# One product for two heads' tails, the reciprocal's argument on ScalarE, and another set of priorities

## The chip, the cores and the metric

The kernel runs on one core of a Trainium2 chip. Its engines work side by side, each through its own queue in order: TensorE (PE in the profile, its weight loads PEld), VectorE (DVE), ScalarE (ACT), GpSimd (POOL), and SyncE (SP), which here only issues DMAs. The metric is the device time of one execution in microseconds, as the median of the timed runs.

## The reference

Three stages follow one another. Attention with 4 batches, 8 heads, 576 positions and head dimension 64: of each row of scores only the 32 largest are kept.

```python
scores = scale * np.matmul(q, k.transpose(0, 1, 3, 2))
kth = np.partition(scores, -top_k, axis=-1)[..., -top_k:-top_k + 1]
scores = np.where(scores >= kth, scores, -1e9)
attn = np.exp(scores - np.max(scores, axis=-1, keepdims=True))
attn = attn / (np.sum(attn, axis=-1, keepdims=True) + 1e-09)
x = np.matmul(attn, v)                       # then heads side by side: 2304 rows of 512
x = np.maximum(np.maximum(x @ w1, x @ w2), x @ w3) @ w_out   # first MoE, 512 -> 768 -> 512
# second MoE: softmax over 8 experts' logits, each row to its best expert:
out[row] = gate[row] * (np.maximum(x[row] @ w1[e], 0) @ w2[e])
```

## The kernel before, in words

Attention works in 72 units. A "full" unit is 128 queries (a block j of 0 to 3) of one pair of heads p; there are 64 of them. A "comb" unit holds the last 64 queries of two pairs; there are 8. The 576 keys fall into four chunks of 128 (KC = 4) and a tail of 64 (TL = 64).

Per unit the steps are: load and split the queries (`q_load`, `q_split`, `q_prep`), TensorE makes scores (`scores`, L751), ScalarE copies them (`s_copy`, L762), VectorE folds the two halves of a row (L820) and finds the 32nd largest by rounds of MAX8 and MATCH_REPLACE8 (L828, L832, L835, L854). `mask` (L874 on ScalarE, L876 on GpSimd) and `expo` (L882 on ScalarE) give weights and, through the accumulator, their sums; `recip` prepares the sum on GpSimd (L937: plus 1e-9, times a scale) and takes its reciprocal on VectorE (L936); from unit 14 on (`early_scale`) GpSimd scales the rows by it (`scale_rows`, L946). `pt` transposes the weights on TensorE (L899, and L913 for both heads' tails at once), ScalarE copies them out (L903, L921).

`av` is the product with v. In a full unit it writes both heads into one PSUM tile, head 0 in partitions 0 to 63 and head 1 in 64 to 127. First come the tails, one product for each head in a quarter of the array (L963, 64 rows by 64 columns), then four chunks by two heads (L967, 128 rows by 64 columns). An f32 product is two records in the trace. `norm` copies the result to the tile xf (L1001), and `x_split` makes two f16 parts of it (L1028, L1033), the input of the first MoE.

v lies in a tile of five slots by two heads (`v_load`, five DMAs for each pair of heads, tile bufs = 5): four chunks, and a slot for the tail, where head 1's tail is loaded twice, once in the lower and once in the upper partitions.

The first MoE (`moe1_steps`) runs on groups of 128 to 320 queries, two a batch and three for the last one; its products (`mm`, L1079, L1119) and evictions (`ev`, L1085, L1088, L1094, L1099) are mixed in with later attention units, and the last groups run alone at the end. Its weights are loaded, decoded and split in the first 150 us (`weight_steps`, steps f, with a check g, L477 and L479). `route_early` computes routing tables for the first three batches (L1383 to L1473) while the last units run. After that come the experts of the second MoE (L1646, L1667).

Up to there the order of work on each engine is made by a planner (`Plan`). Each `add(engine, length, f, reads, writes)` is a step with an assumed length in ns; the planner goes through time and gives each free engine, of the steps that are ready, the one with the smallest key. The key is the step's number in the list less the value of `SOON` under the name of the function that added it; a larger value means sooner. The order is written out; on the chip each engine keeps it and waits where its inputs are late. `at(name, tenant, part, bufs)` names a buffer that a step uses; a new tenant waits until an old one has left.

Of the kernel before, what the change touches and what calls it, by code (L numbers as in the profile page):

```python
# [10 lines left out]
F32 = mybir.dt.float32  # L11
# [5 lines left out]
AF = mybir.ActivationFunctionType  # L17
# [134 lines left out]
def moe_chain_kernel(  # L152
# [112 lines left out]

    xscale = const.tile([128, B + 1, 4], F32, name="xscale")
    REDO = B
# [44 lines left out]
    def whole(redo):  # L312
# [308 lines left out]
        def v_load(b, p):  # L621
            for i, hd in ((0, 0), (0, 1), (1, 0), (1, 1), (2, 1)):
                def f(i=i, hd=hd):
                    if (b, p) not in VT:
                        VT[b, p] = ap_.tile([128, NTT, 2, D], F32, name="v", bufs=5)
                    vt, src = VT[b, p], of_batch(v, b)[2 * p + hd]
                    if i == 0:
                        nc.sync.dma_start(vt[:, 0:KC, hd, :], src[0:KC * 128].rearrange("(c p) d -> p c d", p=128))
                    elif i == 1:
                        nc.sync.dma_start(vt[:TL, KC, hd, :], src[KC * 128:S])  # L630
                    else:
                        nc.sync.dma_start(vt[TL:128, KC, hd, :], src[KC * 128:S])
                add("SP", ISSUE, f, (), [at("v", (b, p), (i, hd), 5)], size=(131072, 16384, 16384)[i])

        def v_max(b):
# [5 lines left out]
            for i in range(4):  # L641
# [11 lines left out]
            add("DVE", 60, lambda: V.tensor_scalar(xscale[:, b, 2:3], xscale[:, b, 1:2], float(2.0 ** -13), None, op0=OP.mult),  # L653
                [at("xs", 0, (b, 0))], [at("xs", 0, (b, 2))])

        def x_descale(b):
# [75 lines left out]
        def bat(u):  # L732
            return u[1]
# [197 lines left out]
        def recip(u):  # L931
            sm, r = at("sm", u, None, 3), at("r", u, None, 2)

            def f():
                RR[u] = ap_.tile([128, 2], F32, name="r", bufs=2)
                V.reciprocal(RR[u], SUM[u])  # L936
            add("POOL", 348, lambda: G.tensor_scalar(SUM[u], SUM[u], 1e-9, xscale[:, bat(u), 2:3], op0=OP.add, op1=OP.mult),  # L937
                [at("xs", 0, (bat(u), 2))], [sm])
            add("DVE", 71, f, [sm], [r])
# [9 lines left out]
        def av(u):  # L949
# [4 lines left out]
            def f():  # L954
                r = RR.pop(u)
                pst = psM.tile([128, 512], F32, name="m")
                ps = pst[:, 0:256].rearrange("p (a b) -> p a b", a=2)
                if full:
                    p = u[3]
                    vt = VT[b, p]  # L960
                    for hd in range(2):
                        rows = slice(hd * TL, (hd + 1) * TL)
                        PE.matmul(ps[rows, 0, :], vt[rows, KC, hd, :], PT[u, 2][rows, 0, :], start=True, stop=False,  # L963
                                  skip_group_check=True)
                    for c in range(KC):
                        for hd in range(2):
                            PE.matmul(ps[hd * 64:(hd + 1) * 64, 0, :], vt[:, c, hd, :], PT[u, hd][:, c, :],  # L967
                                      start=False, stop=(c == KC - 1), skip_group_check=True)
# [3 lines left out]
                else:  # L972
                    for g in range(2):
                        vt = VT[b, u[2] + g]
                        for hd in range(2):
                            o = ps[hd * 64:(hd + 1) * 64, 0, g * TL:(g + 1) * TL]
                            for c in range(KC):
                                PE.matmul(o, vt[:, c, hd, :], PT[u, g][:, c, hd * TL:(hd + 1) * TL],
                                          start=(c == 0), stop=False, skip_group_check=True)
                            PE.matmul(o, vt[:TL, KC, hd, :], PT[u, 2][:TL, g, hd * TL:(hd + 1) * TL],  # L980
                                      start=False, stop=True, skip_group_check=True)
# [5 lines left out]
            vs = [at("v", (b, p), None, 5) for p in ((u[3],) if full else (u[2], u[2] + 1))]  # L987
            add("PE", (1400 if full else 2700) + (0 if early_scale(u) else 230), f,
                vs + [pt_at(u, i) for i in range(3)] + ([] if early_scale(u) else [at("r", u, None, 2)]), [T])

# [4 lines left out]
        def norm(u):  # L995
# [3 lines left out]
            def f():  # L999
                XF[u] = ap_.tile([128, 128], F32, name="xf", bufs=2)  # L1000
                A.activation(XF[u], AV.pop(u)[:, 0, :], AF.Copy)  # L1001
# [5 lines left out]
            def h():  # L1007
                XF[u] = ap_.tile([128, 128], F32, name="xf", bufs=2)
                G.tensor_tensor(XF[u], box["rb"][:, 0, :], box["rb"][:, 1, :], op=OP.mult)
# [46 lines left out]
        def moe1_steps(g):  # L1056
# [72 lines left out]
            for j, off, m in g["tiles"]:  # L1129
# [44 lines left out]
        EARLY = 67  # L1174
        SOON = {"prefetch_first": 215, "q_prep": 190, "k_prep": 130, "scores": 120, "setup_routing": 120, "k_split":
                95, "first_expert": 95, "q_split": 90, "s_copy": 80, "x_split": 70, "g": 60, "pt": 45, "f": 25, "ev": 20,
                "av": 20, "fin": 5, "mask": -5, "expo": -15, "norm": -25, "v_max": -25, "weight_scales": -35, "setup_bias":
                -35, "scale_rows": -45, "q_load": -60, "route_early": -65, "k_load": -70, "mm": -75, "v_load": -105}
        LAG, LAST, STOP = 3, 1, 0
# [615 lines left out]
```

## Time and profile before

| | |
|---|---|
| median of 3 runs | 1018.72 us (1018.18 to 1021.07) |
| the profiled execution | 1023.0 us |
| its span, first to last instruction | 1021.1 us |
| TensorE busy | 924.2 us (91%) |
| VectorE busy | 752.5 us (74%) |
| ScalarE busy | 699.3 us (68%) |
| GpSimd busy | 548.6 us (54%) |
| mean granted TensorE clock | 0.939 |

Busy time is a union: overlapping records of an engine count once. A mean over the span hides the stages, and so the rows below are cut by stage. "Idle before" is the time in which an engine had nothing running ahead of an instruction, and "<-" names what ended it.

### The profile page before, as it was taken

To read this page: it belongs to the slowest core of one execution; us is meant where nothing else is said; L and a number is where in the kernel's file an instruction comes from. 1 tells how busy PE (TensorE), PEld (TensorE's weight loads), DVE (VectorE), ACT (ScalarE), POOL (GpSimd) and SP (SyncE) were. 2 spreads that over 40 slices of the span, in tenths; PEclk is the share of its full clock that TensorE was granted. 3 is DMA by queue.
4 is the path that set the end of the run, shared out by engine and by line. 5 is a ranking of instruction groups with operands and counts; after the bars stand their busy time and mean duration, and the time that the engine had idled before them with its cause. 6 is when DMAs were issued, how large, how long until landed. Compare 5 with 4: busy or idle time off the path is not lost. (4 is left out here: it accounts for less than half of the span.)

```text
span 1021.1 us, 21954 instructions
## 1 busy us (share of the span) xinstructions
PE 924.2 (91%) x7518; PEld 769.0 (75%) x7518; DVE 752.5 (74%) x2510; ACT 699.3 (68%) x1624; POOL 548.6 (54%) x831
## 2 busy tenths in 40 slices
PE   5357599999999999999999999998899899989995
PEld 4245478887778888778888887875797678768883
DVE  7999989999999999999989999996327111331110
ACT  7889889899888999888989888765432222432221
POOL 4678568787767786776876776654210211221000
PEclk8568689999999999999999999998899899989998
DMA  7743230132201123000001000000301521241000
GB/s 188 209 133 108 66 95 16 32 92 66 77 14 33 41 46 100 7 17 30 17 20 40 29 10 2 27 1 9 122 13 53 197 63 42 73 157 50 25 22 27
DMA packets 83795, 60.48 MB, mean 59 GB/s; under 512 B 67009, under 2 KB 67009, under 8 KB 83650
## 3 DMA queue, kind: packets, MB, share of 16 engines
q1 hardware_dynamic: 80770, 49.32, 17.0%
q0 software_dynamic: 2880, 9.44, 2.7%
q8 instruction: 65, 1.06, 0.4%
q14 instruction: 80, 0.66, 0.2%
HBM read 49.30 MB, written 9.44 MB: 58 GB/s over the span
## 5 line engine op out<-in xcount | busy, mean ns | idle before, releaser
L828 DVE MAX8 tk<-wk 128x8 f32<-128x288 f32 x576 | 237.2, 446 | 0.0
L876 POOL TENSOR_TENSOR ss<-mk,ss 128x576 f32<-128x576 bf16 x144 | 185.7, 1297 | 45.5 <-ACT mk L874 44.8
L835 DVE MATCH_REPLACE8 wk<-tk,wk 128x288 f32<-128x288 f32 x432 | 188.2, 441 | 0.0
L874 ACT ACTIVATE mk<-ss,kb 128x576 bf16<-128x576 f32 x144 | 110.6, 780 | 19.2 <-POOL kb L777 19.0
L1647 ACT ACTIVATE hid<-ph 128x512 f32<-128x512 f32 x36 | 21.5, 598 | 140.5 <-PE ph L1646 140.5
L882 ACT ACTIVATE ss<-ss,kb 128x576 f32<-128x576 f32 x144 | 112.0, 779 | 2.8 <-POOL ss L876 2.6
L751 PE MATMUL s<-ks,qt 128*128 128x288 f32 x512 | 95.1, 330 | 19.6 <-ACT ss L762 19.6
L762 ACT ACTIVATE ss<-s 128x576 f32<-128x576 f32 x144 | 93.8, 651 | 21.5 <-PE s L751 20.5
L820 DVE TENSOR_TENSOR wk<-s,ss 128x576 f32<-128x576 f32 x144 | 102.7, 744 | 5.6 <-ACT ss L762 5.6
L946 POOL TENSOR_SCALAR ss<-ss,r,nil 128x576 f32<-128x576 f32 x116 | 95.5, 828 | 17.0 <-DVE r L936 12.5
L1671 POOL DMA_INDIRECT out_dram<-bo,tab x18 | 18.3, 1016 | 158.0 <-ACT bo L1670 150.6
L899 PE MATMUL t<-ident,ss 128*128 128x128 f32 x576 | 89.3, 285 | 10.2 <-ACT ss L882 8.9
L1635 DVE TENSOR_TENSOR bxl<-px,bxh 128x512 fp32r<-128x512 f32 x18 | 12.4, 690 | 115.6 <-ACTq L1683 97.5
L751 PEld LDWEIGHTS s<-ks,qt 128*128 128x128 f32 x512 | 78.2, 208 | 23.9 <-ACT ss L762 21.7
L903 ACT ACTIVATE pt<-t 128x512 f32<-128x512 f32 x144 | 84.3, 597 | 12.5 <-PE t L899 11.2
L899 PEld LDWEIGHTS t<-ident,ss 128*128 128x128 f32 x576 | 67.1, 146 | 19.7 <-ACT ss L882 11.7
L967 PE MATMUL m<-pt,v 128*64 128x128 f32 x1024 | 74.8, 291 | 0.0
L967 PEld LDWEIGHTS m<-pt,v 128*64 128x64 f32 x1024 | 58.6, 144 | 11.9 <-issue 11.9
L1088 DVE SCALAR_TENSOR_TENSOR hb<-m,wfac,hb 128x320 f32<-128x320 f32 (+2 forms) x102 | 49.2, 483 | 16.2 <-PE m L1079 14.9
L1646 PE MATMUL ph<-e1h,bxh 128*128 128x512 f32 x144 | 59.5, 413 | 1.2 <-ACT bxh L1634 0.7
L1667 PE MATMUL py<-e2h,bhh 128*128 128x512 f32 x144 | 58.4, 406 | 1.4 <-ACT bhh L1658 1.4
L832 DVE MAX8 tk<-wk 128x8 f32<-128x288 f32 x144 | 58.6, 442 | 0.0
(309 smaller groups left out, 2672.4 us busy)
## 6 DMA issues: line engine op xcount, KB each, us to landing
raw<-in_moe_w_dram SPq DMA_DIRECT2D x6, 2048.0 KB, 9.6
raw<-in_moe_w_dram SPq DMA_DIRECT2D x18, 512.0 KB, 4.1
kraw<-in_v_dram SPq DMA_DIRECT2D x16, 288.0 KB, 3.9
qraw<-in_q_dram SPq DMA_DIRECT2D x64, 64.0 KB, 2.0
kraw<-in_k_dram SPq DMA_DIRECT2D x32, 128.0 KB, 2.6
v<-in_v_dram SPq DMA_DIRECT2D x32, 128.0 KB, 2.7
x_rows<-row SPq DMA_DIRECT2D x16, 256.0 KB, 2.1
raw<-in_moe_w_out_dram SPq DMA_DIRECT2D x6, 512.0 KB, 4.4
```

Of the source, the lines that this page charges most:

```text
L751: PE.matmul(ST[u][:, hf, t, :HALF], qt[:, i, :], KS[bat(u), p][:, hd, k0:k0 + HALF], start=(n == 0), stop=(n == len(parts) - 1))
L762: A.activation(SS[u][:, :, hf * HALF:(hf + 1) * HALF], ST[u][:, hf, :, :HALF], AF.Copy)
L820: V.tensor_tensor(WK[u][:, :, w, :], ST[u][:, 0, :, :HALF], SS[u][:, :, HALF:S], op=op)
L828: V.max(TK[u][:, t, r * 8:r * 8 + 8], WK[u][:, t, 0, :])
L835: add("DVE", 426, lambda: V.match_replace(WK[u][:, t, 0, :], TK[u][:, t, r * 8:r * 8 + 8], WK[u][:, t, 0, :], NEG), [tk_at(u, (t, r))], [w ...
L874: A.activation(box["m"], SS[u][:, t, :], AF.Relu, bias=KTH[u][:, t, 1:2], scale=-BIG)
L876: add("POOL", 1250, lambda: G.tensor_tensor(SS[u][:, t, :], box["m"], SS[u][:, t, :], op=OP.subtract), [M], rows_at(u, t))
L882: A.activation(SS[u][:, t, :], SS[u][:, t, :], AF.Exp, bias=KTH[u][:, t, 0:1], scale=-scale * UP, accum_out=SUM[u][:, t:t + 1])
L899: PE.transpose(t[:, c, :], SS[u][:, i, c0:c0 + 128], ident)
L903: A.activation(o, box["t"], AF.Copy)
L946: add("POOL", 790, lambda: G.tensor_scalar(SS[u][:, t, :], SS[u][:, t, :], RR[u][:, t:t + 1], nil, op0=OP.mult, op1=OP.add), [at("r", u, N ...
L967: PE.matmul(ps[hd * 64:(hd + 1) * 64, 0, :], vt[:, c, hd, :], PT[u, hd][:, c, :], start=False, stop=(c == KC - 1), skip_group_check=True)
```

## The change

In a full unit the two tail products become one with 128 rows and 128 columns. Its stationary operand is two adjacent slots of v: the first holds head 0's tail in the lower 64 partitions and zeros in the upper, the second zeros in the lower and head 1's tail in the upper. The v tile has a third slot for head 1's tail in the lower partitions, which the comb units use. Two memsets on GpSimd write the zeros. The sum's "plus 1e-9, times a scale" becomes an ACT activation with the scale 2^-13 and the bias 1e-9 times it, the bias computed once a batch on VectorE. The tile xf is taken in `av` rather than in `norm`, and the planner's step of `av` asks for its room; the assumed length of `av` is 1230 for 1400. The table `SOON` has other values, and `recip` has one where it had none (0).

```diff
-    xscale = const.tile([128, B + 1, 4], F32, name="xscale")
+    xscale = const.tile([128, B + 1, 5], F32, name="xscale")
...
-                        VT[b, p] = ap_.tile([128, NTT, 2, D], F32, name="v", bufs=5)
+                        VT[b, p] = ap_.tile([128, 2 * KC + 3, D], F32, name="v", bufs=5)
...
-                        nc.sync.dma_start(vt[:, 0:KC, hd, :], src[0:KC * 128].rearrange("(c p) d -> p c d", p=128))
+                        nc.sync.dma_start(vt[:, hd:2 * KC:2, :], src[0:KC * 128].rearrange("(c p) d -> p c d", p=128))
                     elif i == 1:
-                        nc.sync.dma_start(vt[:TL, KC, hd, :], src[KC * 128:S])
+                        nc.sync.dma_start(vt[:TL, 2 * (KC + hd), :], src[KC * 128:S])
                     else:
-                        nc.sync.dma_start(vt[TL:128, KC, hd, :], src[KC * 128:S])
+                        nc.sync.dma_start(vt[TL:128, 2 * KC + 1, :], src[KC * 128:S])
+            for hd in range(2):
+                add("POOL", 130, lambda hd=hd: G.memset(VT[b, p][(1 - hd) * TL:(2 - hd) * TL, 2 * KC + hd, :], 0.0), (),
+                    [at("v", (b, p), (3, hd), 5)])
...
+            add("DVE", 60, lambda: V.tensor_scalar(xscale[:, b, 4:5], xscale[:, b, 2:3], 1e-9, None, op0=OP.mult),
+                [at("xs", 0, (b, 2))], [at("xs", 0, (b, 4))])
...
-            add("POOL", 348, lambda: G.tensor_scalar(SUM[u], SUM[u], 1e-9, xscale[:, bat(u), 2:3], op0=OP.add, op1=OP.mult),
-                [at("xs", 0, (bat(u), 2))], [sm])
+            x = xscale[:, bat(u)]
+            add("ACT", 75, lambda: A.activation(SUM[u], SUM[u], AF.Identity, bias=x[:, 4:5], scale=x[:, 2:3]),
+                [at("xs", 0, (bat(u), 2)), at("xs", 0, (bat(u), 4))], [sm])
...
-                    for hd in range(2):
-                        rows = slice(hd * TL, (hd + 1) * TL)
-                        PE.matmul(ps[rows, 0, :], vt[rows, KC, hd, :], PT[u, 2][rows, 0, :], start=True, stop=False,
-                                  skip_group_check=True)
+                    PE.matmul(ps[:, 0, :], vt[:, 2 * KC:2 * KC + 2, :], PT[u, 2][:, 0, :], start=True, stop=False,
+                              skip_group_check=True)
...
-            add("PE", (1400 if full else 2700) + (0 if early_scale(u) else 230), f,
-                vs + [pt_at(u, i) for i in range(3)] + ([] if early_scale(u) else [at("r", u, None, 2)]), [T])
+            add("PE", (1230 if full else 2700) + (0 if early_scale(u) else 230), f,
+                vs + [pt_at(u, i) for i in range(3)] + ([] if early_scale(u) else [at("r", u, None, 2)]), [T, at("xf", u, "room", 2)])
...
-        SOON = {"prefetch_first": 215, "q_prep": 190, "k_prep": 130, "scores": 120, "setup_routing": 120, "k_split":
-                95, "first_expert": 95, "q_split": 90, "s_copy": 80, "x_split": 70, "g": 60, "pt": 45, "f": 25, "ev": 20,
-                "av": 20, "fin": 5, "mask": -5, "expo": -15, "norm": -25, "v_max": -25, "weight_scales": -35, "setup_bias":
-                -35, "scale_rows": -45, "q_load": -60, "route_early": -65, "k_load": -70, "mm": -75, "v_load": -105}
+        SOON = {"x_split": 555, "prefetch_first": 370, "g": 200, "k_prep": 150, "q_prep": 130, "scores": 120,
+                "s_copy": 95, "setup_bias": 80, "first_expert": 70, "k_split": 55, "av": 50, "pt": 45, "setup_routing": 40,
+                "q_split": 30, "f": 30, "mask": -5, "expo": -10, "norm": -25, "ev": -30, "recip": -30, "v_load": -45, "v_max":
+                -55, "weight_scales": -55, "scale_rows": -60, "mm": -80, "k_load": -100, "q_load": -100, "route_early": -110}
```

## Rows read from the trace of the kernel before

**Rows 1.** Busy time by stage; columns in the first line, counts in brackets.
```profile
core 0: us, PE busy (x) PEld busy (x) DVE busy (x) ACT busy (x) POOL busy (x), PEclk, DMA share, GB/s
0.00:150.00 150.00, 93.51 (x652) 75.49 (x653) 136.99 (x464) 126.86 (x290) 98.55 (x150) 0.72 0.50 136
150.00:650.00 500.00, 492.74 (x4600) 415.43 (x4599) 484.93 (x1665) 444.77 (x1076) 366.63 (x583) 1.00 0.14 36
650.00:710.00 60.00, 54.09 (x466) 40.73 (x465) 50.67 (x186) 34.81 (x85) 29.73 (x44) 0.94 0.02 6
710.00:765.00 55.00, 50.96 (x703) 47.11 (x702) 17.89 (x39) 23.00 (x53) 14.42 (x18) 0.94 0.19 66
765.00:1021.00 256.00, 232.90 (x1106) 190.21 (x1106) 62.05 (x158) 69.81 (x124) 39.30 (x37) 0.95 0.20 71
```

**Rows 2.** VectorE's waits, 150 to 650 us: total us, times, longest us.
```profile
DVE r L936 <- POOL sm L937: 6.1, 19, 0.6
DVE wk L820 <- ACT ss L762: 2.5, 5, 1.2
```

**Rows 3.** Timeline of TensorE, one full unit's product: start us, us, record.
```profile
419.02 0.30 PE L1079 MATMUL m<-xl,w1h 128*128 128x320 f16 x1
419.15 0.30 PE L1079 MATMUL m<-xh,w1l 128*128 128x320 f16 x1
419.38 0.44 PE L963 MATMUL m<-pt,v 64*64 64x128 f32 x4
419.75 1.09 PE L967 MATMUL m<-pt,v 128*64 128x128 f32 x16
```

**Rows 4.** Timeline of the weight loads of that product, idle before in brackets.
```profile
419.38 0.20 PEld L963 LDWEIGHTS m<-pt,v 64*64 64x64 f32 x4 [0.26 <-ACT hh L1094]
419.75 0.85 PEld L967 LDWEIGHTS m<-pt,v 128*64 128x64 f32 x16 [0.17 <-issue]
```

**Rows 5.** Timeline of TensorE, eight full-array f32 transposes and what follows.
```profile
674.75 1.09 PE L899 MATMUL t<-ident,ss 128*128 128x128 f32 x8
675.68 0.30 PE L1079 MATMUL m<-xh,w1h 128*128 128x320 f16 x1
```

**Rows 6.** Tail products (L963) by stage: PE busy and records, PEld, clock, DMA.
```profile
0.00:150.00 150.00, 5.63 (x40) 2.43 (x40) 0.72 0.50 136
150.00:650.00 500.00, 20.47 (x188) 9.22 (x188) 1.00 0.14 36
650.00:690.00 40.00, 1.74 (x16) 0.78 (x16) 1.00 0.02 8
690.00:720.00 30.00, 1.56 (x12) 0.74 (x12) 0.89 0.09 28
```

**Rows 7.** Groups by line: busy us, mean ns | idle before, releasers.
```profile
L937 POOL TENSOR_SCALAR sm<-sm,xscale 128x2 f32<-128x2 f32 x72 | 19.3, 268 | 71.2 <-ACT ss L882 64.5 <-PE t L725 2.5 <-PE m L1138 2.0
...
L882 ACT ACTIVATION_READ_ACCUMULATOR ss<-ss,kb 128x1 f32 x144 | 29.0, 202 | 0.0
...
L515 POOL MEMSET mod<- 128x20 int32 x1 | 0.1, 108 | 0.0
```

**Rows 8.** TensorE's waits, 680 to 730 us.
```profile
PE m L1462 <- DVE scratch L1557: 2.5, 1, 2.5
PE m L1079 <- DVE hb L1088: 1.6, 1, 1.6
```

**Rows 9.** VectorE's groups by line, 669 to 691.5 us, three of routing.
```profile
L1421 DVE TENSOR_SCALAR sel<-jf,rank_p 128x128 bf16<-128x128 f32 x15 | 4.8, 323 | 0.0
...
L1416 DVE CAST rank_i<-rank 128x15 int32<-128x15 f32 x1 | 1.1, 1118 | 0.0
L1417 DVE TENSOR_SCALAR rank_i<-rank_i 128x15 int32<-128x15 int32 x1 | 1.0, 965 | 0.0
```

**Rows 10.** VectorE's waits, 0 to 150 us.
```profile
DVE gram L479 <- PE m L477: 3.5, 1, 3.5
DVE wk L820 <- ACT ss L762: 2.4, 1, 2.4
DVE r L936 <- POOL sm L937: 1.8, 3, 0.8
```

More of the change, by code (lines that the diff above doesn't have):

```diff
@@ L955, in f @@
                 r = RR.pop(u)
+                XF[u] = ap_.tile([128, 128], F32, name="xf", bufs=2)
                 pst = psM.tile([128, 512], F32, name="m")
@@ L960, in f @@
                     vt = VT[b, p]
-                    for hd in range(2):
-                        rows = slice(hd * TL, (hd + 1) * TL)
-                        PE.matmul(ps[rows, 0, :], vt[rows, KC, hd, :], PT[u, 2][rows, 0, :], start=True, stop=False,
-                                  skip_group_check=True)
+                    PE.matmul(ps[:, 0, :], vt[:, 2 * KC:2 * KC + 2, :], PT[u, 2][:, 0, :], start=True, stop=False,
+                              skip_group_check=True)
                     for c in range(KC):
                         for hd in range(2):
-                            PE.matmul(ps[hd * 64:(hd + 1) * 64, 0, :], vt[:, c, hd, :], PT[u, hd][:, c, :],
+                            PE.matmul(ps[hd * 64:(hd + 1) * 64, 0, :], vt[:, 2 * c + hd, :], PT[u, hd][:, c, :],
                                       start=False, stop=(c == KC - 1), skip_group_check=True)
@@ L977, in f @@
                             for c in range(KC):
-                                PE.matmul(o, vt[:, c, hd, :], PT[u, g][:, c, hd * TL:(hd + 1) * TL],
+                                PE.matmul(o, vt[:, 2 * c + hd, :], PT[u, g][:, c, hd * TL:(hd + 1) * TL],
                                           start=(c == 0), stop=False, skip_group_check=True)
-                            PE.matmul(o, vt[:TL, KC, hd, :], PT[u, 2][:TL, g, hd * TL:(hd + 1) * TL],
+                            PE.matmul(o, vt[:TL, 2 * (KC + hd), :], PT[u, 2][:TL, g, hd * TL:(hd + 1) * TL],
                                       start=False, stop=True, skip_group_check=True)
@@ L999, in f @@
             def f():
-                XF[u] = ap_.tile([128, 128], F32, name="xf", bufs=2)
                 A.activation(XF[u], AV.pop(u)[:, 0, :], AF.Copy)
@@ L1007, in h @@
             def h():
-                XF[u] = ap_.tile([128, 128], F32, name="xf", bufs=2)
                 G.tensor_tensor(XF[u], box["rb"][:, 0, :], box["rb"][:, 1, :], op=OP.mult)
```

## The prediction

> **What bounds the kernel now.** I read first the busy time by stage [rows 1]. From 0 to 150 us VectorE is busy 137.0 of 150 us and TensorE 93.5; TensorE has too little to do there, and its granted clock averages 0.72. From 150 to 650 us both are full: TensorE 492.7 of 500, VectorE 484.9, while ScalarE has 55.2 us free and GpSimd 133.4. From 650 to 710 the last units of attention end with holes in TensorE (54.1 of 60); from 710 to 765 TensorE alone works off the first MoE's last groups (51.0 of 55); the last 256 us are the experts, which the change does not touch. So TensorE's work sets the end from 150 to 765, with VectorE close behind: a saving on TensorE becomes time only if VectorE can also go faster, and of that the waits tell. VectorE idles 15.1 us of the 500, and its largest wait there is the reciprocal waiting for GpSimd's sum, 6.1 us in 19 places; the next, for ScalarE's copies of scores, is 2.5 [rows 2]. Last I read one product with v record by record [rows 3 to 5], because the change works there.
>
> **The product with v.** It removes, in each of the 64 "full" units, four 64x64 records (two products, two records each) and puts two 128x128 records in their place; the sixteen 128x64 records behind them stay. The records of the MoE before start 0.13 us apart, so the tail could have started at 419.28; it starts at 419.38, and the 128x64 records start at 419.75 [rows 3]. The tails take 0.47 us of TensorE, 0.10 of it at the entry. Inside, the four weight loads take 0.20 and 0.17 is a pause before the next form [rows 4]. New is a full-array f32 product that no row shows. The nearest are eight transposes of the same form, which take 0.93 us to the next instruction, 0.116 a record [rows 5]; two records make 0.23. One change of form is left, full array to 128x64. I price it as the one entry that is seen from the full array, 0.10. So 0.33 against 0.47, 0.135 us saved a unit.
>
> Bounds: if the one switch left costs both the 0.10 at the entry and the 0.17 pause, the new way takes 0.50 and loses 0.03; if it costs nothing, it saves 0.23. I keep 0.135 since its row is the one with a full-array record in front. Units count by stage: 40 records before 150 us are 10 units, then 188, 16 and 12 make 47, 4 and 3 [rows 6]. The 54 after 150 us lie where TensorE is full: 54 x 0.135 = 7.3 us (-1.6 to 12.4). The first 10 hide beside idle TensorE and count nothing.
>
> The Trainium skill (TensorEngine Tiling (Array Packing), Key Properties) says that a change of tiling mode drains the engine; by that rule the switch taken away is the gain, and the pause above agrees. The same page (Theoretical Speedup) speaks against the change: two products small in both dimensions may run side by side in the array, and one block-diagonal product gives that up. By it only the drains would differ, the lower bound above; that is part of a rival below.
>
> **The sum's scale and offset.** GpSimd loses 72 instructions of 0.268 us, 19.3 us, and 71.2 us of standing at the head of its queue for ScalarE [rows 7]; it was not the bound, so by itself that is worth nothing. ScalarE gains 72 activations on two columns. No row shows one that small; the one-column read of the accumulator takes 0.202 us [rows 7], so up to 14.5 us, of which 47 units' 9.5 fall in the 500 us in which 55.2 are free. Hidden; uncovered it is a rival's price. The new activation follows the exponentials on its own engine and waits for nobody else. Behind it stand masks and copies for TensorE.
>
> VectorE's reciprocal now waits for ScalarE without the detour. Behind it stand the top-k instructions, so every wait there costs VectorE directly. Up to 150 us VectorE sets the pace, and this wait is 1.8 us [rows 10]: I count it whole, 1.8 us. From 150 to 650 us the same 6.1 us is not added to TensorE's saving but makes it possible: TensorE there saves 47 x 0.135 = 6.3 us, and VectorE must shed as much of its 15.1 idle. If the wait only moves to ScalarE, both come to nothing, and if ScalarE is later than GpSimd was they turn into a loss (below). Four more VectorE scalings of one column in all are under a microsecond beside its free 13.0 in the start [rows 1].
>
> **Zeros and the layout of v.** Two memsets on each of 16 tiles, 32 in all, on GpSimd. The nearest, a 128x20, took 0.108 us, at most some 4 us, under the 19.3 that leave. A memset may wait for the tile's last reader; behind it stand the mask products, with 133.4 us of room. The five v loads per pair keep their count and size. Nothing, 0 to 2 us if a memset stalls the mask at the first batch.
>
> **The priorities.** They count steps of the list, some sixty a unit. Cost taken: nothing, with ends from rows.
> - Routing goes 45 steps later, most of a unit. From 669 to 691.5 it takes turns with the last top-k on VectorE, 4.8 us of selections and 2.1 for two conversions [rows 9]. Behind the top-k it frees VectorE, but TensorE has the routing's product in its own queue and waited 2.5 us for it, and 1.6 for an eviction behind it [rows 8]. Both gone: 4.1 us; doubled: as much lost.
> - The weights' check comes 140 steps sooner. VectorE waits 3.5 us for it once in the start [rows 10]: from 3.5 us gained to the same lost, if another product holds it up.
> - Loads on SP: v 60 steps sooner, k 30 and q 40 later, modality loads (9, small) 115 sooner, all past the weight pieces. DMA is busy 0.50 of the first 150 us and 0.14 after [rows 1]; q and k are wanted later than they land except at the first units. 0 to 2.4 us lost, the one wait of a fold for scores there [rows 10].
> - MoE evictions go 50 later, MoE products only 5 later. They still lead the products by 50, so no bank stays full: nothing, or at worst the eviction wait of 1.6 us in each of nine groups, 14 us, which I hold unlikely.
> - x_split 485 sooner, and the product with v now asks for room in xf: the two go together, 0. The product with v 30 sooner, queries' split and transposes 60 later, score copies 25 sooner, the first expert's load 155 sooner (wanted only by the experts): an order among steps that are ready, 0, at worst the folds' wait for scores doubled, 2.5 us [rows 2].
>
> **Sum.** 7.3 + 1.8 = 9.1 us. The profiled execution took 1023.0 us (span 1021.1), so it would take 1013.9. It is 4.3 above the median 1018.72 of the timed runs, and the change is taken from that: 1009.6.
>
> **Rivals.**
> A, larger gain: routing behind the last top-k closes TensorE's holes (4.1 us), and the check's wait goes (3.5). 1018.7 - 9.1 - 7.6 = 1002.0. For it: both waits are single events that a new order can miss. Against: the order is written from lengths, and what takes long on the chip can stall a queue in another place. 0.15.
> B, no change: TensorE's saving turns into idle, since VectorE at 97% holds the pace and its wait passes from GpSimd to ScalarE; or the block product saves nothing, because the packed one already ran side by side. Left are the 7 units after 650 us, 0.9 us: 1017.8, or with the lower bound and the start's 1.8, about 1018.5. For it: VectorE's 97%. Against: the 6.1 us are the largest part of its 3%. 0.20.
> C, slower: ScalarE becomes the late one. The activation of 0.20 us stands in front of masks and score copies, and VectorE's folds wait for those. On the path in 54 units it costs 10.9 us, with TensorE's saving lost: 1018.7 + 10.9 - 0.9 - 1.8 = 1026.9. It decides where ScalarE's free time per unit (55.2 us over 47 units, 1.2 us) is gone; against it, that is six times the activation; for it, an engine in order has its free time where it waits and not where it is needed. 0.13.
>
> **Numbers.** Forecast 0.52, A 0.15, B 0.20, C 0.13. Some 3 us (0.3%) is what a measurement can tell from no change. Faster: forecast and A, 0.67; same: B, 0.20; slower: C, 0.13. The range goes from 1000 (A with the upper bound of the product partly in it) to 1020 (B); C and the far end of A lie outside. The forecast's own range is 1004 to 1015.
>
> **What would show it.** Right: one pair of records of about 0.23 us in front of the 128x64 ones, TensorE in 150 to 650 us still at 98%, the reciprocal's wait under 2 us, ScalarE's busy share about 91%, the expert stage starting about 9 us sooner and lasting 256. B: TensorE's busy time falls with the stage's length unchanged. C: VectorE's folds waiting more than 8 us for score copies. A: no hole at 690 to 700 us. The forecast is wrong if the first 150 us shift by more than 4 us either way, or if the experts start later than 765.

## The result, and the profile after

The changed kernel takes 1031.04 us (median of 4 runs, 1030.93 to 1031.56) where the kernel before took 1019.38 beside it: a ratio of 1.0114 with a 95% interval of 1.0097 to 1.0132, 11.7 us slower. The forecast was 1009.6, faster; the time lies outside its range. The profiled execution took 1031.09 us (span 1029.3), close to its median; that of before lies 4.3 above its own, so the profiles stand only 8.2 us apart.

Busy time by stage, after, in the columns of [rows 1]:
```profile
0.00:150.00 150.00, 89.18 (x598) 72.96 (x600) 132.09 (x443) 126.54 (x291) 95.85 (x147) 0.74 0.50 135
150.00:650.00 500.00, 490.79 (x4471) 418.30 (x4467) 482.77 (x1664) 455.87 (x1123) 350.62 (x545) 1.00 0.14 35
650.00:710.00 60.00, 56.48 (x488) 44.80 (x488) 56.62 (x205) 41.30 (x100) 31.18 (x45) 0.97 0.04 12
710.00:765.00 55.00, 47.72 (x621) 42.97 (x617) 20.80 (x46) 22.79 (x52) 14.44 (x18) 0.88 0.21 66
765.00:1021.00 256.00, 240.75 (x1228) 195.50 (x1224) 63.10 (x161) 71.98 (x131) 40.09 (x39) 0.98 0.20 70
```
Against [rows 1] the first 150 us hold 4.9 us less VectorE work (132.1 for 137.0): attention is behind from the start. In the dense 500 us TensorE and VectorE are busy as before within 2.2 us, ScalarE 11.1 us more and GpSimd 16.0 less. VectorE's fold (L820 before, L825 after) of unit 12 begins at 162.6 us instead of 151.2, that of unit 18 at 217.5 instead of 209.2, of unit 42 at 429.1 instead of 419.4, of unit 71 at 682.2 instead of 676.4; the first product of the experts starts at 773.5 instead of 766.3. So the delay arises before unit 12, where it is 11.4 us. By unit 71 half of it is won back (5.8 us left), and at the experts it is 7.2 us.

VectorE's waits after, 0 to 150 us and then 150 to 650 (total us, times, longest), beside [rows 10] and [rows 2]:
```profile
DVE r L941 <- ACT sm L943: 5.5, 3, 2.8
DVE bd L332 <- ACT scratch L429: 2.6, 3, 1.2
DVE scratch L378 <- POOL w3l L462: 1.4, 1, 1.4
DVE gram L479 <- PE m L477: 1.1, 1, 1.1
```
```profile
DVE hb L1091 <- PE m L1082: 6.5, 13, 1.0
DVE r L941 <- ACT sm L943: 3.5, 9, 0.7
DVE logits L1166 <- PE m L1147: 2.5, 6, 0.8
```
The weights' check costs 1.1 us in the start for 3.5, as its new priority should make it, and the reciprocal 3.5 in the dense stage for 6.1. But the reciprocal waits 5.5 us in the start for 1.8, three times only; waits for 2.6 and 1.4 us stand beside it, and in the dense stage VectorE's evictions of the first MoE wait 6.5 us for TensorE's products, where before had:
```profile
DVE hb L1088 <- PE m L1079: 1.3, 3, 0.6
```

Summed record by record up to the last MAX8 on a row of scores (L828 before, L833 after), VectorE had 662.2 us of own work and 29.3 idle before, 660.2 and 36.5 after: the 5.2 us by which this ends later come from 7.2 us more idle time, with 2.0 us less work. From there to the experts it is 76.8 for 74.8 us. TensorE in 730 to 745 us, first before and then after, shows where:
```profile
730.00:745.00 15.00, 14.71 (x233) 14.52 (x233) 6.20 (x14) 4.80 (x14) 3.50 (x7) 0.90 0.06 20
```
```profile
730.00:745.00 15.00, 8.69 (x105) 8.37 (x105) 7.89 (x12) 6.40 (x15) 4.08 (x5) 0.60 0.34 108
```
```profile
PE m L1082 <- ACT row L1157: 5.4, 1, 5.4
```
The last line is TensorE's largest wait after, 680 to 745 us: a first-MoE product held for a copy on ScalarE (L1157), with the granted clock at a mean of 0.60 in 730 to 745 us. Before has a wait for the same copy, and it was its largest there:
```profile
PE m L1144 <- ACT row L1154: 3.0, 1, 3.0
```
The holes that the forecast saw near 700 [rows 8] have moved and not closed.

The product now stands in the trace as two records. One of them, to be read beside [rows 3] and [rows 4] (TensorE, then its weight loads; 128x128 f32 transposes run ahead here and not MoE products):
```profile
403.83 0.46 PE L968 MATMUL m<-pt,v 128*128 128x128 f32 x2
404.22 1.09 PE L972 MATMUL m<-pt,v 128*64 128x128 f32 x16
```
```profile
403.80 0.30 PEld L968 LDWEIGHTS m<-pt,v 128*128 128x128 f32 x2
404.21 0.85 PEld L972 LDWEIGHTS m<-pt,v 128*64 128x64 f32 x16
```
From the pair to the 128x64 records it is 0.39 us here, where the two old products take 0.37 [rows 3]; the next section shows that the gain depends on what TensorE did before. And the sum on ScalarE: mean of its 72 activations, and one in the timeline with what follows:
```profile
L943 ACT ACTIVATE sm<-sm,xscale 128x2 f32<-128x2 f32 x72 | 28.2, 393 | 1.6 <-DVE xscale L658 1.1
```
```profile
405.60 0.40 ACT L943 ACTIVATE sm<-sm,xscale 128x2 f32<-128x2 f32 x1
405.88 0.78 ACT L879 ACTIVATE mk<-ss,kb 128x576 bf16<-128x576 f32 x1
```
It takes 0.39 us, and the next instruction starts 0.28 after it, where the plan counts 75 ns.

### The profile page after: what moved, and what is told of

Read it like the earlier page. It is cut to its first block, busy times and chain, and to the rows that moved or that the text cites. A ratio compares the mean times of both kernels' runs of the same rounds, so it can differ in the third digit from the quotient of the medians.

```text
span 1029.3 us, 21749 instructions
## 1 busy us (share of the span) xinstructions
PE 924.9 (90%) x7390; PEld 774.5 (75%) x7390; DVE 755.4 (73%) x2514; ACT 718.5 (70%) x1696; POOL 532.2 (52%) x791
## 5 line engine op out<-in xcount | busy, mean ns | idle before, releaser
L833 DVE MAX8 tk<-wk 128x8 f32<-128x288 f32 x576 | 236.9, 447 | 0.0
L825 DVE TENSOR_TENSOR wk<-s,ss 128x576 f32<-128x576 f32 x144 | 102.4, 743 | 2.4 <-ACT ss L767 2.3
L904 PEld LDWEIGHTS t<-ident,ss 128*128 128x128 f32 x576 | 69.6, 148 | 31.3 <-ACT ss L887 19.4
L1102 POOL TENSOR_TENSOR hl<-hb,hh 128x320 f16<-128x320 f32 (+2 forms) x54 | 36.6, 677 | 55.1 <-ACT hh L1097 53.2
L1082 PE MATMUL m<-xh,w2h 128*128 128x320 f16 (+2 forms) x204 | 56.0, 280 | 6.7 <-ACT row L1157 5.4
```

The source lines that it names most:

```text
L825: V.tensor_tensor(WK[u][:, :, w, :], ST[u][:, 0, :, :HALF], SS[u][:, :, HALF:S], op=op)
L833: V.max(TK[u][:, t, r * 8:r * 8 + 8], WK[u][:, t, 0, :])
L904: PE.transpose(t[:, c, :], SS[u][:, i, c0:c0 + 128], ident)
```

## The experiments

Each ran beside the kernel before on the same chip; ratios are to that, with 95% intervals. "Order kept" means that the planner saw the same steps and lengths as in the kernel named. By the traces VectorE's 2510 records then stand in the same order but for 0 to 3 (9 in r_same, beside the four scalings that it adds). A record counts as moved when it lies outside the longest sequence that is in the same order in both traces. The theories were that the time follows TensorE's work, ScalarE's new activation, or the order as a whole.

**The parts alone, in the order of before.** p_same has the block-diagonal product and the zeros, written in the step that loads v:
```diff
+                        for z in range(2):
+                            G.memset(vt[(1 - z) * TL:(2 - z) * TL, 2 * KC + z, :], 0.0)
...
+                    PE.matmul(ps[:, 0, :], vt[:, 2 * KC:2 * KC + 2, :], PT[u, 2][:, 0, :], start=True, stop=False, ...)
```


> The kernel before with the one block-diagonal product alone. The planner still sees 1400 ns and no memset, so the order of the planned work stays (the zeros are written where the last of the five v loads is issued). Theory S (the new priorities spoil the first 160 us): the trace after shows 1.475 us for a product with v against 1.620, and 54 units lie where TensorE is full, so 4 to 8 us faster than before, about 1013. Theory R (the sum on ScalarE makes reciprocals late): the same 1013, since no sum is moved. Theory D (VectorE holds the pace whatever TensorE saves): within 2 us of before, 1017 to 1020.

1018.34 for 1019.79, ratio 0.9984 (0.9974 to 0.9994). One product of it:
```profile
417.19 0.30 PE L1079 MATMUL m<-xh,w1l 128*128 128x320 f16 x1
417.33 0.38 PE L963 MATMUL m<-pt,v 128*128 128x128 f32 x2
417.64 1.09 PE L967 MATMUL m<-pt,v 128*64 128x128 f32 x16
```
From the MoE record to the 128x64 records it is 0.45 us where [rows 3] show 0.60. Over the full units of 170 to 650 us that stand behind an MoE product, the median from the record before to the instruction after the product is 1.475 us for 1.620: 0.145 saved, for 0.135 forecast. But these are 17 units. Behind 64x64 transposes of the queries the same product is longer than the old two, first before and then p_same:
```profile
539.46 0.50 PE L725 MATMUL t<-identr,qx 64*128 64x64 f32 x4
539.89 0.44 PE L963 MATMUL m<-pt,v 64*64 64x128 f32 x4
540.26 1.09 PE L967 MATMUL m<-pt,v 128*64 128x128 f32 x16
```
```profile
537.43 0.50 PE L727 MATMUL t<-identr,qx 64*128 64x64 f32 x4
537.86 0.49 PE L963 MATMUL m<-pt,v 128*128 128x128 f32 x2
538.28 1.09 PE L967 MATMUL m<-pt,v 128*64 128x128 f32 x16
```
The pair takes 0.42 us to the 128x64 records for 0.37, and loses 0.05. Taken unit by unit, from the record before to the first 128x64 record, 19 of the 47 units of 150 to 650 us save 0.11 to 0.145 us (most behind an MoE or a score product), 11 save 0.07 (behind 128x128 transposes of the queries), and 17 lose 0.01 to 0.12, most of them 0.05 (behind 64x64 transposes, or where TensorE had waited for the product's inputs). The sum is 2.6 us, where 0.135 each makes 6.3.

From unit 18 to unit 54 the folds run parallel to those of before, 2.0 us ahead at both ends. The products there save 1.2 us in all, too little for two profiles to tell. Nor is the lead of 2.0 us the product's: tail_twice below, with more tail work than before, has it too at unit 18. The timed gain, 1.6 us (0.6 to 2.6), is of the size of what TensorE saved; where it comes in is not shown.

tail_twice keeps the old tails and issues them twice:
```diff
-                    for hd in range(2):
+                    for hd in (0, 1, 0, 1):
```


> The kernel before, its order kept, with the two tail products of every full unit issued twice (the second pair starts the sum anew, so nothing else changes): four more records a unit, some 0.2 to 0.37 us of TensorE, 13 to 24 us over 64 units. Theory T (TensorE sets the pace from 150 us on, as the forecast had it): 11 to 20 us slower, 1029 to 1038. Theory D (VectorE sets it, and a TensorE that looks 98% busy has room in it): 0 to 6 us slower, 1018 to 1024, with VectorE's idle time up by no more than that.

Timed 1028.45 for 1018.39, 1.0096 (1.0068 to 1.0124), between what the two theories expected. By the profile a unit costs 0.218 us more TensorE time (tail 0.584 for 0.366), and the folds fall back from 2.1 us ahead at unit 18 to 2.6 behind at unit 54: 4.7 us over 36 units, some 32 of them full, 0.147 each. So two thirds of the added work count: as far as two profiles tell, TensorE is near its limit there and has some room. By the timed median it is more, 9.8 us of the 11.8 that the trace has added behind 150 us. (The profiled run took 1024.29, the lowest of its six; the rest of the timed loss is not seen in it.)

r_same moves the sum to ScalarE, emitted where GpSimd's stood:
```diff
-            add("POOL", 348, lambda: G.tensor_scalar(SUM[u], SUM[u], 1e-9, xscale[:, bat(u), 2:3], op0=OP.add, op1=OP.mult),
+            add("POOL", 348, lambda: A.activation(SUM[u], SUM[u], AF.Identity, bias=x[:, 4:5], scale=x[:, 2:3]),
```


> The kernel before with the sum's scale and offset on ScalarE alone, issued at the place in the order where GpSimd's stood; the planner does not know of it. Theory S: within 2 us of before, 1017 to 1021, VectorE's waits for the sum 4 to 10 us in all against 7.9. Theory R: 4 to 9 us slower, 1023 to 1028, with the reciprocals' waits at 12 us or more. Theory D: a little faster or the same, 1016 to 1020, because VectorE's wait for GpSimd goes.

1031.85, 1.0109 (1.0092 to 1.0127). VectorE's waits, 0 to 650 us, first p_same, then r_same:
```profile
DVE r L938 <- POOL sm L939: 7.9, 22, 0.8
```
```profile
DVE r L938 <- ACT sm L940: 18.1, 30, 2.2
```
In ScalarE's queue the sum stands behind other work, most often a copy of queries or of transposed weights, and the reciprocal is late by up to 2.2 us. Without a new place in that queue the edit costs 11 us, more than any of the theories had; a new order must give the new place.

p_nosum_same takes the wait away: the product, and from unit 14 on no sum step at all (GpSimd's row scaling applies the scale).
```diff
+            if early_scale(u):
+                add("POOL", 348, lambda: None, [at("xs", 0, (bat(u), 2))], [sm])
...
-            ... RR[u][:, t:t + 1], nil, op0=OP.mult, op1=OP.add),
+            ... RR[u][:, t:t + 1], xscale[:, bat(u), 0:1], op0=OP.mult, op1=OP.mult),
```


> The kernel before, its order kept, with the block-diagonal product and, for the 58 units that scale rows early, no sum step at all: the reciprocal is taken of the plain sum and the power-of-two scale goes into the second operand of the row scaling on GpSimd, where a constant stood (the 1e-9 is left out there). Theory D (VectorE's waits set the pace, and its largest is the reciprocal's): the waits of 6.1 us between 150 and 650 us fall to 2 or less and the kernel takes 4 to 9 us less than before, 1010 to 1015. Theory T (TensorE sets the pace): the same as the product alone, 1017 to 1019.

1017.84 for 1018.87, 0.9989 (0.9977 to 1.0001). The wait I held to be the key to TensorE's saving is gone but for the first units; 0 to 650 us:
```profile
DVE r L938 <- POOL sm L942: 1.5, 2, 0.8
```
VectorE's idle time up to the last top-k is still 29.1 us for 29.3: waits of other names stand in its place.

**Parts of the change, with the order planned anew.** s_only has the new table `SOON` and nothing else:
```diff
-        SOON = {"prefetch_first": 215, "q_prep": 190, "k_prep": 130, "scores": 120, ...
+        SOON = {"x_split": 555, "prefetch_first": 370, "g": 200, "k_prep": 150, "q_prep": 130, ...
```


> The kernel before with the new priorities alone (old product, sum on GpSimd). Theory S: slower by 8 to 14 us, 1027 to 1033, and the fold of unit 12 begins about 11 us later than the 151.2 us of before. Theory R: within 3 us of before, 1016 to 1022, unit 12 within 3 us. Theory D: as theory S or the same; it does not tell.

1034.95, 1.0146 (1.0128 to 1.0163), above the 1027 to 1033 of theory S. Its fold of unit 4 begins at 66.3 us, near after's 67.5, where before's begins at 60.4: the new priorities alone bring a delay in the start. They are not needed for it: pr and p_plan below, planned with the old table, begin unit 12 at 161.6 and 159.2 us for 151.2. Its largest wait of VectorE, 0 to 650 us, has the name of after's second largest (6.5 us there):
```profile
DVE hb L1088 <- PE m L1079: 12.6, 16, 2.2
```

pr is the changed kernel with the old `SOON`:
```diff
-        SOON = {"x_split": 555, "prefetch_first": 370, ...
+        SOON = {"prefetch_first": 215, "q_prep": 190, ...
```


> The changed kernel with the old priorities: product, memsets, room for xf and sum on ScalarE, planned with their lengths. Theory S: 4 to 9 us faster than before, 1010 to 1015, unit 12 beginning within 3 us of 151.2. Theory R: slower than before by 2 us or more, 1021 to 1028, with the loss where reciprocals wait. A third reading, that any newly planned order of this list costs or gains several us in the start by chance: anything from 1008 to 1028, with unit 12 shifted by more than 3 us for reasons that are not the reciprocal's.

1051.73, 1.0296 (1.0276 to 1.0317). ps is the changed kernel with the sum as a GpSimd step again:
```diff
-            add("ACT", 75, lambda: A.activation(SUM[u], ...
+            add("POOL", 348, lambda: G.tensor_scalar(SUM[u], SUM[u], 1e-9, ...
```


> The changed kernel with the sum back on GpSimd (product, memsets, room for xf and the new priorities stay). Alone, the sum on ScalarE cost 11 us at the old order and the new priorities 14. Theory R (the sum's 0.39 us activation is what makes the changed kernel slow, and the priorities only order the rest): 1016 to 1022, reciprocals waiting under 5 us in all. Theory S (the new priorities are worse wherever they stand): 1030 to 1036, with VectorE waiting for TensorE's MoE products 6 us or more. If both add: about 1024.

1042.5, 1.0229 (1.0209 to 1.025). p_plan is before with the product planned as in the change and the old `SOON`:
```diff
+                add("POOL", 130, lambda hd=hd: G.memset(VT[b, p][(1 - hd) * TL:(2 - hd) * TL, 2 * KC + hd, :], 0.0), (), ...
...
-            add("PE", (1400 if full else 2700) + ..., [T])
+            add("PE", (1230 if full else 2700) + ..., [T, at("xf", u, "room", 2)])
```


> The kernel before with the product part as it is in the change, planned: 1230 ns, memsets as steps, room for xf asked by the product; old priorities, sum on GpSimd. With the order kept the product alone gained 1.6 us. Theory N (new orders cost by themselves): slower than before by 3 us or more, 1023 to 1040. Theory X (room for xf holds the product back at the old priority of x_split): slower too, 1025 to 1040, and the first 160 us are not to blame but the folds' waits for scores later on. Theory R (the loss of product and sum together, 32 us, is the sum's): 1016 to 1020.

1042.21, 1.0234 (1.0212 to 1.0255). pr, ps and p_plan all came out above every range expected. VectorE's waits, 0 to 650 us, of pr, then of ps:
```profile
DVE r L941 <- ACT sm L943: 14.8, 21, 2.5
DVE wk L825 <- ACT ss L767: 14.3, 11, 2.7
```
```profile
DVE wk L823 <- ACT ss L765: 14.2, 9, 5.7
```
The same product that gains 1.6 us in p_same loses 23 in p_plan, by being planned and by taking xf in `av` (which alone costs 3.2 us, l_xfroom below). The new priorities are not bad for the changed program, they take back 18.5 us of pr's loss by the ratios; but a part taken out of the change and the rest planned anew makes it slower, clearly in pr and ps, while s_only's interval overlaps the change's. Table, lengths and steps look fitted to one another; no run shows more of that.

after_280 tells the planner that the ScalarE sum is longer:
```diff
-            add("ACT", 75, lambda: A.activation(SUM[u], ...
+            add("ACT", 280, lambda: A.activation(SUM[u], ...
```


> The changed kernel with the planner told 280 ns for the sum's activation in place of 75 (the trace: the next ScalarE instruction starts 0.279 us after it). Theory L (the loss comes from the planner's wrong length, so ScalarE runs behind the order): 4 to 9 us faster than the changed kernel, 1022 to 1027, the reciprocals' waits at 4 us or less against 8.9. Theory R (ScalarE's time itself is the loss): within 3 us of 1031. Theory N (a newly planned order moves the time by several us whatever it knows): anything from 1020 to 1045, with the reciprocals' waits not following the time.

1031.7, 1.0125 (1.0105 to 1.0145). The right length in the plan doesn't win the loss back. That the wrong one cost nothing is not shown, since this order is a new one too (9% of VectorE's records moved against after).

**An order alone.** Is a new order in itself so dear? Five kernels change what the planner is told, and no instruction (l_xfroom also takes the tile xf in another place): the length of one GpSimd step 150 to 160, of a mask 667 to 660, of the product 1400 to 1230, two empty steps where the change has memsets, and the room in xf.
```diff
-            add("POOL", 150, f, [tk_at(u, None)], [at("kb", u, None, 3)])
+            add("POOL", 160, f, [tk_at(u, None)], [at("kb", u, None, 3)])
```


> The kernel before, not one instruction changed: only the planner is told 160 ns for a small GpSimd step that it knew as 150, and it writes another order (about a third of the planned lines of VectorE and ScalarE stand elsewhere). Theory N (the order before is an unusually good one, and any new order adds waits in VectorE's queue): 6 to 25 us slower, 1025 to 1045, VectorE idle 36 us or more until the last top-k against 29.3. Theory P (the product's own planning terms are to blame: 1230 ns, memsets, room for xf): within 4 us of before.


```diff
-            add("ACT", 667, f, [kb_at(u)] + rows_at(u, t), [M])
+            add("ACT", 660, f, [kb_at(u)] + rows_at(u, t), [M])
```


> The same with one other length: the mask on ScalarE planned with 660 ns for 667, no instruction changed. Theory N: 6 to 25 us slower, 1025 to 1045, and not by the same amount as with the other length. Theory P: within 4 us of before.


```diff
-            add("PE", (1400 if full else 2700) + (0 if early_scale(u) else 230), f,
+            add("PE", (1230 if full else 2700) + (0 if early_scale(u) else 230), f,
```


> The kernel before with the planner told 1230 ns for the product with v and nothing else; the product itself stays the old one. Theory N: 6 to 25 us slower, as with the two lengths that have nothing to do with the change (7 and 11 us). Theory X: within 4 us. A third, that a product planned too short makes TensorE run late: slower, with VectorE's waits for MoE products at 5 us or more against 1.9.


```diff
+            for hd in range(2):
+                add("POOL", 130, lambda hd=hd: None, (), [at("v", (b, p), (3, hd), 5)])
```


> The kernel before with two empty steps of 130 ns per v tile on GpSimd in the plan, where the change has its memsets; no instruction is added. Theory N: 6 to 25 us slower. Theory X: within 4 us.


```diff
-                vs + [pt_at(u, i) for i in range(3)] + ..., [T])
+                vs + [pt_at(u, i) for i in range(3)] + ..., [T, at("xf", u, "room", 2)])
```


> The kernel before with one planning term of the product part alone: the tile xf is taken in the product with v and the planner's step asks for its room; no instruction changes, and little of the order (about 100 of VectorE's lines). Theory X (the room is what cost 24 us where the product was planned): 10 us slower or more, 1028 and up. Theory N (any new order costs, the more the more of it is new): within 5 us of before.

| kernel | VectorE records moved | median us | ratio |
|---|---|---|---|
| l_xfroom | 5 (0.2%) | 1021.97 | 1.0031 (1.0015 to 1.0048) |
| l_mask660 | 88 (4%) | 1024.89 | 1.0070 (1.0050 to 1.0090) |
| l_kth160 | 192 (8%) | 1028.08 | 1.0104 (1.0086 to 1.0122) |
| l_memstep | 222 (9%) | 1031.42 | 1.0113 (1.0084 to 1.0142) |
| l_av1230 | 253 (10%) | 1036.78 | 1.0160 (1.0127 to 1.0192) |
| the change | 361 (14%) | 1031.04 | 1.0114 (1.0097 to 1.0132) |

Ten nanoseconds in the plan, on an engine with 133.4 of the dense 500 us free [rows 1], cost 10.6 us. In the three slowest of the five the waits that come are folds waiting for score copies, 12.5 to 14.2 us; l_kth160, 0 to 650 us:
```profile
DVE wk L820 <- ACT ss L762: 12.5, 11, 2.4
```
Before has 5.0 there. In l_mask660 and l_xfroom, with 5.7 and 5.1, the loss lies elsewhere and was not followed. All five are slower, and the more, the more records moved; beyond these five the rule fails (the change moves more than l_av1230 and costs less, p_plan moves 256 and costs more). All eleven kernels here whose order was planned anew are slower than before, by 0.3 to 3.0%. So the order of before looks like an unusually good one for the chip, as far as eleven draws tell, and why it is good is not shown.

**The order of the change, with the parts undone.** Three kernels keep the planner's steps of the changed kernel and put old instructions into them. a_pool_same has the sum on GpSimd again, at the new place:
```diff
-            add("ACT", 75, lambda: A.activation(SUM[u], SUM[u], AF.Identity, bias=x[:, 4:5], scale=x[:, 2:3]),
+            add("ACT", 75, lambda: G.tensor_scalar(SUM[u], SUM[u], 1e-9, x[:, 2:3], op0=OP.add, op1=OP.mult),
```


> The changed kernel, its order kept, with the sum's scale and offset back on GpSimd at the place where ScalarE's activation stood; the planner does not know of it. Theory R (ScalarE's activation costs as at the order before, 11 us): 5 to 12 us faster than the changed kernel, 1019 to 1026, reciprocals waiting 3 us or less. Theory N (the order is what costs; this order was made for the sum on ScalarE): within 3 us of 1031, or slower, since GpSimd then stands in its queue for ScalarE.

1027.13 for 1017.15, 1.0101 (1.0083 to 1.0119): the change's ratio within the intervals, so the sum's engine is worth nothing clear in this order. a_old_same has the two tail products again:
```diff
-                    PE.matmul(ps[:, 0, :], vt[:, 2 * KC:2 * KC + 2, :], PT[u, 2][:, 0, :], ...)
+                    for hd in range(2):
+                        rows = slice(hd * TL, (hd + 1) * TL)
+                        PE.matmul(ps[rows, 0, :], vt[rows, 2 * KC + hd, :], PT[u, 2][rows, 0, :], ...)
```


> The changed kernel, its order kept, with the two 64x64 tail products in place of the block-diagonal one. Theory D (VectorE sets the pace): 0 to 3 us slower than the changed kernel, 1031 to 1034. Theory T (TensorE sets the pace from 150 us on, as predicted): 7 to 9 us slower, 1038 to 1040.

1035.42 (1030.13 to 1036.52), 1.0166 (1.0142 to 1.0190). By the ratios that is 5.3 us slower than the change, between what the two theories expected, and its trace has 5.1 us more TensorE time around the 55 products behind 150 us: here TensorE's time seems to count in full. (The profiled run took 1031.72, near the lowest of its five.) order_alone undoes both and leaves the memsets and the new scaling out, so that only the order, the layout of v and the place where xf is taken are left of the change (beside the edits of the last two):
```diff
-                add("POOL", 130, lambda hd=hd: G.memset(VT[b, p][(1 - hd) * TL:(2 - hd) * TL, 2 * KC + hd, :], 0.0), (),
+                add("POOL", 130, lambda: None, (),
```


> Every instruction of the kernel before, in the order that the change wrote: two 64x64 tail products, the sum on GpSimd, no memsets and no new VectorE scaling; only the tile of v keeps its new layout and xf is taken in av. By theory W (the new order puts waits into VectorE's queue whatever stands in it, and the parts have small effects of their own) it costs 12 to 19 us, no less than the change itself (11.7): the change without its product took 1.0166 and the change without its ScalarE sum 1.0101 against 1.0114, so 1.0114 + 0.0052 - 0.0013 = 1.0153, about 1034; and VectorE's fold of unit 12 begins 8 to 14 us later than before. By theory E (the new activations on ScalarE and the product, not the order, are what costs) it comes within 4 us of the kernel before, 1015 to 1023.

1031.42 for 1019.2, 1.0117 (1.0096 to 1.0138), the change's own ratio within the interval. It lies at the lower edge of the 12 to 19 us expected (11.9 by its ratio) and at three times the 4 us of the theory that blames the new instructions. The 1.0153 that the two runs before it add up to lies outside its interval, so the parts don't simply add, and the 5.3 us of a_old_same is not borne out by it. Its fold of unit 12 begins at 164.2 us (before 151.2, after 162.6), its first expert product starts at 774.9 (773.5). VectorE's waits of it, 0 to 150 and 0 to 650 us:
```profile
DVE r L941 <- POOL sm L943: 8.3, 2, 5.4
```
```profile
DVE r L941 <- POOL sm L943: 11.4, 11, 5.4
DVE hb L1093 <- PE m L1084: 7.9, 17, 0.9
DVE logits L1168 <- PE m L1149: 4.0, 7, 1.0
```
These waits have the names that they have in the changed kernel. Its VectorE records stand in after's order but for 6. Instruction for instruction the old work, in the new order, loses what the change loses: the order is the cause, and the new instructions in it come out even (11.9 us alone, 11.7 with them). Of what else stays of the change, the layout of v costs nothing in p_same, and the place of xf at most 3.2 us (l_xfroom).

## Why the prediction was wrong

**The step that failed is "The priorities ... Cost taken: nothing".** I priced the new table edit by edit, by the one wait that each moved step has in the trace, and found nothing. What the table changes is the whole order, 14% of VectorE's records, on a chip where engines wait in written order; and the new lengths and steps would have changed it without any new table (p_plan, l_av1230). The price is 11.9 us by order_alone. The ends that I did price did not foresee it. The largest, 14 us for evictions that hold up TensorE, did not come: TensorE waits 3.0 us for them in 680 to 745 us, for 1.6. The waits that did grow were small in the trace of before: reciprocals in the start (5.5 us for 1.8), evictions that wait for products (6.5 for 1.3), a copy ahead of the last products (5.4 for 3.0). My list also leaves `recip` out, whose own step moves 30 places later; whether the reciprocals' wait comes from that no run shows. (It has the score copies 25 steps sooner, too, where the table says 15.)

**The product's term was mis-sized: "The 54 after 150 us lie where TensorE is full: 54 x 0.135 = 7.3 us".** The 0.135 was read from one unit behind an MoE product, and there it was right: 0.145, with one of two changes of form gone as priced. But TensorE comes to the product from other work as well, and there the pair of records saves 0.07 us or loses 0.05. In the order of before the 47 units of the dense stage save 2.6 us and not 6.3.

**"TensorE's work sets the end from 150 to 765" is neither shown nor refuted.** Of the work that tail_twice adds, two thirds count by its profile and more by its median. Of work taken away, p_same's timed 1.6 us are of the size of what was saved, and a_old_same and order_alone differ on it. The busy share can't tell: records of 0.30 us start 0.13 apart [rows 3], so an engine may stand still some 0.17 us behind each of them and show no gap, and in p_same TensorE is busy 491.9 of the 500 us for 492.7. The Trainium skill (Perfetto Trace Analysis, Identifying the Most-Contended Engine) says that the busy share of matmul records is not a good measure of how near TensorE is to its limit, since they are pipelined, and names the busy share of weight loads, beside the work done per time, in its place. That share was 83% in [rows 1] and 84% in p_same; no run here shows what share would be full. Whether VectorE's 97%, which I read against myself, sets the pace is open too: no run took work from VectorE.

**"this wait is 1.8 us [rows 10]: I count it whole" failed.** In the start the wait grew to 5.5. And taking it away in the dense stage is worth little: in p_nosum_same other waits filled VectorE's idle time to 29.1 us of 29.3.

**The sum on ScalarE** was priced at 0.202 us, the nearest row, and takes 0.39. The Trainium skill (ScalarE: Activation LUTs, What ACT_TABLE_LOAD costs) gives 186 ns, 0.833 ns an element and about 93 ns for each operand read per partition, with instructions overlapping by 93: 374 ns and 281 to the next, by an estimate from it. The trace agrees, 388 ns in the median and 280. That it is hidden fits the new place: the change is 0.13% slower than a_pool_same by the ratios, inside their intervals. At the old place (r_same) it is not hidden.

**Of the rivals,** C named a time of 1026.9, the nearest, but not the cause: folds wait 2.3 us for score copies in the start, as before, and not the 8 that it asked for. So its nearness is luck. B, that TensorE's saving turns into idle time, is not shown, since TensorE saved little in p_same. No rival was an order that is worse as a whole. Of my signs, TensorE's 98% and ScalarE's 91% came as forecast. The pair in front of the 128x64 records takes 0.31 us to them, and not about 0.23, even behind an MoE product, and the reciprocal's wait is 5.5 us in the start and 3.5 in the dense stage (limit 2); the fold of unit 12, which stood just behind the first 150 us, shifted by 11.4 us (limit 4), and the experts started at 773.5 (limit 765).

**Open.** Up to the experts the profiles differ by 7.2 us, and the medians by 11.7. The experts' stage has the same 1101 TensorE records in before, p_same, after and order_alone and lasts 254.9 us in the profile of before, which is 4.3 above its median, 255.8 after and 251.0 in p_same, with mean granted clocks of 0.95, 0.97 and 0.97. Whether the other 4.5 us are there, by the clock, the profiles can't settle. Nor was any better order looked for; the new table with the new sum and the old product was not tried. p_same is the only one of these versions that is clearly under the kernel before, by 1.6 us.

## What to carry to other kernels

Where a program writes the order for engines that wait in it, price a change of lengths or priorities as a new draw of the order: first change one length by a few nanoseconds, with no instruction changed, and see what that costs (7.1 us for 7 ns and 10.6 for 10 here). Try each instruction change with the old order kept, which shows its own worth, and plan anew only if that worth exceeds the spread. Price a changed product behind each kind of work that comes before it, and not from one place. And call no engine the bound by its busy share: double its disputed work once, take it away once, and sum in the trace how much was really taken away.

## What the runs showed of the hardware

A ScalarE activation on 128x2 f32 with bias and scale both read per partition takes 0.39 us, where the same step takes 0.27 on GpSimd [rows 7]; the next ScalarE instruction starts 0.28 us after it. One block-diagonal f32 product takes, from its start to that of the 128x64 records, 0.31 us behind an f16 MoE product, 0.39 behind 128x128 f32 transposes and 0.42 behind 64x64 ones or after most waits (p_same); four packed 64x64 records take 0.37 behind all of these (before). Behind the MoE product it is also entered without the extra 0.10 us.
